# Redrawing the instruction order of an attention-and-MoE kernel: head, steady step, loads and tail at once

## The chip, the cores and the metric

One NeuronCore of a Trainium2 chip. Time is device time in microseconds (us), the median of several executions. The trace is of one execution under the hardware profiler. All executions that are compared are fast unless it is said. Ratios are the mean time of one kernel's fast runs over that of the other's of the same rounds, so they are not quite the ratio of the medians that are quoted. PE is TensorE, DVE VectorE, ACT ScalarE, POOL GpSimd, SP the engine whose queue issues the transfers.

## The reference

```python
f = 1 / (1 + exp(-f_logit))                       # 4 batches, 8 heads, 768 positions, 48 wide
for t in range(S):
    state = f[:, :, t, :, None] * state + outer(k[:, :, t], v[:, :, t])
    y[:, :, t] = q[:, :, t] @ state               # per head
x  = y as [3072 tokens, 384]
out = maximum(x @ w1, x @ w2) @ w_out             # d_ff = 1024
```

## The kernel before

The sequence is cut into 24 steps of 128 positions of one batch. The maximum is rewritten as x @ w2 plus relu(x @ (w1 - w2)), so the kernel prepares `wd = w1 - w2` and `w2o = w2 @ w_out` once, at the start, and every step then runs the same short list of operations. An operation of step i is written as a name and a number; a text lists them in program order, and each engine takes its own in that order. Who waits for whom follows from the data.

```python
PROLOGUE = """setup 0 ... lf 1 lf 0 lq 0 ... """      # head, written out
STEP     = """st -4  d0 -1  cum 1  a 0  ed 1 ... """  # step i; the number is added to i
EPILOGUE = """ ... """                                # tail, written out

# loads (SP): lf lk lq lv of f, k, q, v, 192 KB each, nine buffers of each; out: a store
# ACT:  e, ln (log of the gate), ei, ed (exp of the running sum), fl, x, g0, g1 (relu)
# PE:   cum, tr (transposes of kp and qp), a (scores), y, xT, sa, d0, d1 (x @ wd), o0, o1 (into out)
# DVE:  am (scores x mask), tre, xTe, ob (out of PSUM), tmp, v (v to bf16), w2Te
def m_kp(i, eng):                                     # kp = k * ei; "kp" on POOL, "kpv" on DVE
    eng.tensor_mul(s["kp"][:, :, 0:D], ld[i]["k"], s["ei"]...)
def m_qp(i, eng):                                     # qp = q * ed; "qp" on POOL, "qpv" on DVE
    eng.tensor_mul(s["qp"][:, :, 0:D], ld[i]["q"], s["ed"]...)
def m_st(i):                                          # state, two halves, always on POOL
    nc.gpsimd.tensor_mul(st_b[...], tmp[...], fl[...])
def sub_wd(j, eng=nc.vector):                         # "wd" on DVE, "wdp" on POOL
    eng.tensor_sub(wd[:, j, :], w1_f[:, j, :], w2_f[:, j, :])
def v_v(i):
    nc.vector.tensor_copy(vb, ld[i]["v"]...)          # f32 to bf16
```

## Time and profile before

| | before |
|---|---|
| time | 146.09 us (145.61 to 146.18) |
| PE busy | 130.0 us of a span of 144.2 |
| step in the steady part | 4.975 us, PE never idle |
| last idle time of PE before that part | 0.61 us, at y of step 3 |
| DMA | 28.3 MB in 129 transfers, busy from the second slice on |

How to read it: PE sets the end from 37 us on. What can change the time is when PE becomes dense, and whether something breaks it afterwards. The prediction below shows the lines.

### The profile page before, as it was taken

To read this page: it belongs to the slowest core of one execution; us is meant where nothing else is said; L and a number is where in the kernel's file an instruction comes from. 1 tells how busy PE (TensorE), PEld (TensorE's weight loads), DVE (VectorE), ACT (ScalarE), POOL (GpSimd) and SP (SyncE) were. 2 spreads that over 40 slices of the span, in tenths; PEclk is the share of its full clock that TensorE was granted. 3 is DMA by queue.
4 is the path that set the end of the run, shared out by engine and by line. 5 is a ranking of instruction groups with operands and counts; after the bars stand their busy time and mean duration, and the time that the engine had idled before them with its cause. 6 is when DMAs were issued, how large, how long until landed. Compare 5 with 4: busy or idle time off the path is not lost.

```text
span 144.2 us, 4442 instructions
## 1 busy us (share of the span) xinstructions
PE 130.0 (90%) x1820; PEld 101.3 (70%) x1820; DVE 104.4 (72%) x191; ACT 88.6 (61%) x199; POOL 54.6 (38%) x80
## 2 busy tenths in 40 slices
PE   0197499999899999999999999999999999999981
PEld 0044366677678877887887788778878877777771
DVE  7234988766989778877977797798779777976520
ACT  3572548877387566658566765766585667663440
POOL 8320060230556066236524632652364246362000
PEclk9999999999999999999999999999999999999999
DMA  4999999999999999999898999989899998971111
GB/s 93 271 362 386 341 303 154 188 188 140 206 174 196 188 213 221 173 227 233 166 203 183 215 208 210 219 181 196 182 198 222 190 251 180 225 223 57 59 55 55
DMA packets 104612, 28.60 MB, mean 198 GB/s; under 512 B 100368, under 2 KB 103568, under 8 KB 104592
## 3 DMA queue, kind: packets, MB, share of 16 engines
q1 hardware_dynamic: 104592, 28.32, 90.1%
q8 instruction: 14, 0.23, 0.7%
q14 instruction: 6, 0.05, 0.1%
HBM read 23.59 MB, written 4.72 MB: 196 GB/s over the span
## 4 chain that ended last, share of the span: by engine, by line
PE 72%; SPq 19%; DMA 4%; DVE 1%; issue 1%; ACT 0%
PE o L352 25%; PE d L334 22%; SPq L148 13%; PE tr L249 6%; PE a L267 5%; SPq L153 5%; DMA vt<-in_v_dram 4%; PE y L312 3%; PE y L307 2%; PE xtp L322 2%; PE cum L214 2%; PE sa L281 2%; SPq L157 1%; PE o L373 1%; DVE am L272 1%
## 5 line engine op out<-in xcount | busy, mean ns | idle before, releaser
L242 POOL TENSOR_TENSOR qp<-qt,ed 128x384 bf16<-128x384 f32 x22 | 22.3, 1013 | 61.7 <-ACT ed L226 31.6
L334 PE MATMUL d<-xT,wd 128*128 128x128 bf16 x576 | 40.6, 220 | 0.8 <-DVE xT L326 0.4
L352 PE MATMUL o<-wo,gT 128*128 128x384 bf16 x184 | 37.4, 325 | 0.0
L334 PEld LDWEIGHTS <-wd 128*128 128x128 bf16 x576 | 34.4, 114 | 3.8 <-DVE wd L175 0.6
L341 ACT ACTIVATE gT<-d 128x512 bf16<-128x512 f32 x48 | 29.0, 604 | 10.1 <-PE d L334 10.0
L272 DVE TENSOR_TENSOR am<-a,mask 128x1024 bf16<-128x1024 f32 x24 | 29.4, 1224 | 0.7 <-PE a L267 0.7
L296 POOL TENSOR_TENSOR st<-tmp,fl 64x192 bf16<-64x192 f32 x40 | 25.5, 638 | 1.6
L326 DVE COPY xT<-xtp 128x384 bf16<-128x384 bf16 x24 | 8.6, 358 | 21.1 <-PE xtp L322 21.1
L352 PEld LDWEIGHTS <-gT 128*128 128x128 bf16 x184 | 16.1, 97 | 9.1 <-ACT gT L341 0.2
L226 ACT ACTIVATE ed<-cum 128x384 f32<-128x384 f32 x24 | 11.8, 493 | 16.5 <-PE cum L216 13.1
L258 DVE COPY trs<-tr 128x1024 bf16<-128x1024 bf16 (+1 forms) x27 | 17.0, 631 | 2.9 <-PE tr L249 1.1
L317 ACT CAST x<-y 128x384 bf16<-128x384 f32 x24 | 11.5, 478 | 12.3 <-PE y L312 12.3
L352 PE MATMUL o<-w2o,xT 128*128 128x384 bf16 x69 | 15.0, 326 | 0.0
L201 ACT ACTIVATE e<-ft 128x384 f32<-128x384 f32 x24 | 12.5, 525 | 3.4 <-DMA ft<-in_f_logit_dram 3.4
L237 DVE TENSOR_TENSOR kp<-kt,ei 128x384 bf16<-128x384 f32 x23 | 14.1, 613 | 0.5 <-ACT ei L222 0.5
L214 PE MATMUL cum<-ell,ut 128*128 128x384 bf16 x24 | 8.1, 340 | 6.8 <-ACT ell L205 6.8
L205 ACT ACTIVATE ell<-e 128x384 bf16<-128x384 f32 x24 | 12.5, 524 | 0.7
L357 DVE COPY ob<-o 128x384 f32<-128x384 f32 x23 | 12.6, 548 | 0.0
L222 ACT ACTIVATE ei<-cum 128x384 f32<-128x384 f32 x24 | 12.1, 503 | 0.0
L312 PE MATMUL y<-vb,am 128*128 128x48 bf16 x192 | 11.3, 183 | 0.8 <-DVE am L272 0.6
L312 PEld LDWEIGHTS <-am 128*128 128x128 bf16 x192 | 9.6, 96 | 3.1 <-DVE am L272 1.4
L289 DVE TENSOR_TENSOR tmp<-sa,st 128x384 f32<-128x384 f32 x20 | 10.9, 546 | 0.0
(56 smaller groups left out, 167.6 us busy)
## 6 DMA issues: line engine op xcount, KB each, us to landing
ft<-in_f_logit_dram SPq DMA_DIRECT2D x24, 192.0 KB, 4.2
qt<-in_q_dram SPq DMA_DIRECT2D x24, 192.0 KB, 4.6
kt<-in_k_dram SPq DMA_DIRECT2D x24, 192.0 KB, 4.2
vt<-in_v_dram SPq DMA_DIRECT2D x24, 192.0 KB, 4.5
out_dram<-ob SPq DMA_DIRECT2D x23, 192.0 KB, 3.6
w_f<-in_moe_w_dram SPq DMA_DIRECT2D x6, 512.0 KB, 6.9
wo_f<-in_moe_w_out_dram SPq DMA_DIRECT2D x2, 768.0 KB, 8.4
out_dram<-obl SPq DMA_DIRECT2D x2, 96.0 KB, 1.6
```

The source lines that it names most:

```text
L148: nc.sync.dma_start(out=t, in_=SRC[name][b, :, sl, :].rearrange("h p d -> p h d"))
L201: nc.scalar.activation(e, ld[i]["f"].rearrange("p h d -> p (h d)"), AF.Exp, scale=-1.0)
L237: eng.tensor_mul(s["kp"][:, :, 0:D], ld[i]["k"], s["ei"].rearrange("p (h d) -> p h d", h=H))
L242: eng.tensor_mul(s["qp"][:, :, 0:D], ld[i]["q"], s["ed"].rearrange("p (h d) -> p h d", h=H))
L258: nc.vector.tensor_copy(s["tr"][:, n:n + len(sel)], psum.pop(("tr" + sel, i)))
L272: nc.vector.tensor_mul(am.rearrange("p o n c -> p (o n) c"), psum.pop(("a", i)).rearrange("p o n c -> p (o n) c"), mask)
L296: nc.gpsimd.tensor_mul(st_b[b][(c + 1) % 2][r, :, e], st[i]["tmp"][r, :, e], st[i]["fl"][r, :].unsqueeze(2).to_broadcast([DP, NP, D]))
L312: nc.tensor.matmul(out=y[:, ds], lhsT=am[:, o, p, :], rhs=vb[:, ds], start=(c == 0), stop=(c == 0 or o == 1))
L334: nc.tensor.matmul(out=ps[:, n, :], lhsT=wd[:, j, ff(f)], rhs=st[i]["xT"][:, j, :], start=(j == 0), stop=(j == JG - 1))
L341: nc.scalar.activation(s["g"][:, half * 4:half * 4 + 4, :], psum.pop(("d", half, i)), AF.Relu)
L352: nc.tensor.matmul(out=psum["o", i], lhsT=l() if callable(l) else l, rhs=r, start=(n == 0), stop=(n == len(mms) - 1))
L357: nc.vector.tensor_copy(t, psum.pop(("o", i)))
```

## The change

Its intent: draw the orders of all engines anew for the head (seven steps), the steady step and the tail, around the same first sixteen loads (the two loads of w_out trade places) and with their landing times from the trace. No operation of the kernel changes; nine `warm` matmuls, which kept the array busy early, go. The texts differ in nearly every line; the parts that matter are:

```diff
 PROLOGUE   (cut; ... marks cuts)
-... cum 0  cum 1  lw1 0  w2ca 2  warm 5 ... warm 3  warm 1 ... w2ca 1  w2T 0 ...
+... cum 0  ei 0  ln 1 ... w2ca 2 ... w2c 0  lq 1  w2c 1  kpv 0  w2T 5 ... w2T 1  w2Te 4  cum 1 ...
-... lf 3  wdp 0  woc 3  xT 0  trke 1  w2o 5  xTe 0 ... wd 2 ... wd 1
+... tmp 0 ... st 0 ... kp 1 ... wdp 0 ... wd 2  xT 0 ... xTe 0 ... wd 1
-... qp 2 ... kpv 2 ... kpv 3 ... qp 3 ... qp 4 ... kpv 4 ... qp 5 ... kpv 5
+... qp 2 ... kpv 2 ... kp 3  g1 1  v 2 ... qpv 3 ... qp 4 ... kp 4 ... kp 5 ... qp 5
-... lf 5 ... lv 3  lq 4  lk 4  lk 5  lv 4  lq 5  lv 5 ... lf 9  out 0  lv 8  out 1  lk 9
+... lv 3  lq 4  lk 4  lf 5  lv 4  lv 5  lk 5 ... lf 11  lv 7  lq 8  lf 10  lk 8  lq 10  lq 9  lv 11  lv 8  lk 9
 STEP
-st -4  d0 -1  cum 1  a 0  ed 1  d1 -1  g0 -1  am 0  lv 2  qp 1  fl 1  ei 1  lq 3  g1 -1
-o0 -1  kpv 1  y 0  tmp -2  lk 3  o1 -1  x 0  e 2  xT 0  tr 1  ln 2  out -4  xTe 0  sa -1
-tre 1  ob -1  lf 4  v 1
+st -4  cum 1  d0 -1  ei 1  a 0  g0 -1  d1 -1  am 0  fl 1  g1 -1  o0 -1  tmp -2  ed 1  y 0
+e 2  kpv 1  o1 -1  x 0  qpv 1  ln 2  xT 0  tr 1  xTe 0  sa -1  tre 1  ob -1  v 1  lv 5  lq 7
+lk 7  out -4  lf 9
 EPILOGUE
-(five steps written out) ... lo 0  lo 2  lob0 0  lo 1 ... lo 3  lout 0  lob1 0 ... lout 1
+... lo 1  lo 3  lob1 0  lo 0  lo 2  lout 1  lob0 0  lout 0
```

More of the change, by code (lines that the diff above doesn't have):

```diff
@@ L17 @@
 PROLOGUE = """
-setup 0  setup 2  setup 1  lf 1  lf 0  lq 0  lw2 2  lk 0  lw2 0  lw2 1  lv 0  lwo 0  e 0
-lwo 1  e 1  ln 1  lk 1  ln 0  cum 0  cum 1  lw1 0  w2ca 2  warm 5  ei 0  lw1 2  fl 0  ed 0
-kp 0  ei 1  qpv 0  ed 1  fl 1  lw1 1  w2c 0  warm 3  warm 1  lq 1  w2ca 1  w2T 0  lf 2  w2T 7
-trk 0  w2Te 7  trq 0  w2T 4  trke 0  w2Te 0  trqe 0  w2T 5  w2T 1  a 0  lv 1  am 0  w2Te 1
-w2Te 4  v 0  lq 2  woc 2  w2T 2  y 0  w2Te 2  w2Te 5  woc 0  w2T 6  lk 2  w2T 3  woc 1  w2Te 6
-w2o 2  kpv 1  w2o 1  x 0  w2Te 3  trk 1  lf 3  wdp 0  woc 3  xT 0  trke 1  w2o 5  xTe 0
@@ L24 @@
-w2o 4  w2o 7  w2o 10  lv 2  w2o 8  w2o 0  sa 0  wd 2  w2o 11  w2o 3  lk 3  w2oe 2  w2o 6
-w2oe 1  w2o 9  wd 1  w2oe 0  lq 3  qpv 1  d1 0  lf 4  e 2  trq 1  d0 0  ln 2  trqe 1  tmp 0
-lf 5  a 1  g0 0  v 1  cum 2  am 1  ed 2  lv 3  o0 0  g1 0  qp 2  ei 2  y 1  fl 2  lq 4  kpv 2
-o1 0  x 1  xT 1  trk 2  xTe 1  lk 4  e 3  trq 2  trke 2  d0 1  ln 3  trqe 2  ob 0  lk 5
-cum 3  a 2  v 2  ed 3  d1 1  g0 1  am 2  lv 4  ei 3  g1 1  o0 1  kpv 3  lq 5  y 2  qp 3
-o1 1  x 2  fl 3  xT 2  lv 5  e 4  tr 3  xTe 2  ln 4  sa 1  d0 2  tre 3  lf 6  ob 1  cum 4
@@ L30 @@
-g0 2  a 3  d1 2  ed 4  lk 6  v 3  am 3  ei 4  g1 2  o0 2  lq 6  qp 4  e 5  tmp 1  y 3  fl 4
-o1 2  x 3  st 0  lf 7  kpv 4  ln 5  xT 3  tr 4  xTe 3  sa 2  lk 7  cum 5  tre 4  d0 3  ob 2
-a 4  lv 6  v 4  g0 3  d1 3  am 4  ei 5  ed 5  lv 7  g1 3  o0 3  qp 5  tmp 2  fl 5  y 4  kpv 5
-lq 7  o1 3  x 4  st 2  xT 4  lq 9  e 6  tr 5  xTe 4  st 1  sa 3  ln 6  d0 4  tre 5  lf 8
-ob 3  cum 6  g0 4  a 5  v 5  d1 4  ed 6  am 5  lq 8  ei 6  qp 6  g1 4  o0 4  tmp 3  fl 6
-out 2  e 7  y 5  kpv 6  o1 4  x 5  lk 8  ln 7  xT 5  tr 6  xTe 5  sa 4  lf 9  d0 5  tre 6
@@ L36 @@
-ob 4  cum 7  g0 5  a 6  out 0  v 6  d1 5  ed 7  am 6  ei 7  lv 8  qp 7  g1 5  o0 5  tmp 4
-y 6  kpv 7  out 1  o1 5  x 6  st 3  fl 7  xT 6  tr 7  lk 9  e 8  xTe 6  sa 5  ln 8  tre 7
-lk 10  ob 5  v 7  lf 10
+setup 0  setup 2  setup 1  lf 1  lf 0  lq 0  lw2 2  lk 0  lw2 0  lw2 1  lv 0  lwo 1  e 0
+lwo 0  e 1  ln 0  lk 1  cum 0  ei 0  ln 1  lw1 0  ed 0  w2ca 2  lw1 2  lw1 1  w2c 0  lq 1
+w2c 1  kpv 0  w2T 5  lf 2  w2T 4  w2Te 5  w2T 1  w2Te 4  cum 1  qpv 0  w2T 3  ed 1  tr 0
+lv 1  w2Te 3  woc 3  v 0  w2Te 1  w2T 6  ei 1  tre 0  w2T 2  fl 1  fl 0  sa 0  w2Te 6  w2T 0
@@ new lines @@
+tmp 0  lq 2  woc 0  w2T 7  w2Te 0  a 0  st 0  w2Te 7  woc 1  w2Te 2  lk 2  w2o 2  am 0  woc 2
+kp 1  w2o 1  w2o 0  lf 3  w2o 3  wdp 0  y 0  trk 1  x 0  w2o 4  w2o 5  lk 3  wd 2  xT 0
+w2o 8  w2o 7  w2o 11  xTe 0  w2o 6  lv 2  wd 1  w2oe 2  w2o 10  w2o 9  w2oe 1  lq 3  qpv 1
+w2oe 0  d1 0  trke 1  trq 1  lf 4  e 2  d0 0  trqe 1  ln 2  a 1  g0 0  lv 3  v 1  cum 2
+am 1  fl 2  g1 0  o0 0  lq 4  ed 2  ei 2  y 1  qp 2  lk 4  o1 0  x 1  kpv 2  xT 1  trk 2
+lf 5  e 3  xTe 1  trq 2  trke 2  d0 1  ln 3  trqe 2  ob 0  lv 4  a 2  g0 1  cum 3  am 2
@@ new lines @@
+d1 1  fl 3  ei 3  lv 5  kp 3  g1 1  v 2  o0 1  lk 5  ed 3  y 2  qpv 3  o1 1  x 2  lf 6  e 4
+xT 2  tr 3  ln 4  xTe 2  sa 1  lq 5  d0 2  tre 3  ob 1  cum 4  lf 7  a 3  v 3  ed 4  d1 2
+g0 2  am 3  qp 4  lk 7  ei 4  fl 4  g1 2  o0 2  tmp 1  kp 4  lq 6  e 5  y 3  o1 2  x 3  st 1
+ln 5  lk 6  v 4  xT 3  tr 4  xTe 3  cum 5  tre 4  d0 3  lf 8  ei 5  ob 2  sa 2  a 4  g0 3
+v 5  lv 6  d1 3  kp 5  ed 5  am 4  lq 7  e 6  o0 3  g1 3  tmp 2  y 4  out 2  qp 5  o1 3
+x 4  fl 5  xT 4  st 2  lf 9  e 7  tr 5  xTe 4  ln 6  sa 3  d0 4  tre 5  lf 11  ob 3  cum 6
@@ new lines @@
+a 5  tmp 3  ed 6  lv 7  d1 4  g0 4  am 5  fl 6  ln 7  lq 8  ei 6  o0 4  qpv 6  g1 4  y 5
+kp 6  lf 10  o1 4  x 5  st 3  xT 5  tr 6  lk 8  xTe 5  cum 7  tre 6  d0 5  ei 7  lq 10  ob 4
+fl 7  sa 4  a 6  g0 5  lq 9  v 6  d1 5  ed 7  am 6  e 8  qp 7  lv 11  g1 5  o0 5  kpv 7
+ln 8  y 6  lv 8  tmp 4  o1 5  x 6  e 9  lk 9  xT 6  tr 7  xTe 6  cum 8  tre 7  d0 6  lf 13
+ob 5  sa 5  a 7  v 7  lv 9  lq 11  lq 12  out 0  lk 10  lq 14  lv 10  lf 12  lk 11  lk 12
+lv 12  out 1  out 5  out 4  lf 14  lf 15  lq 13  lk 14  lk 13
@@ L47 @@
 EPILOGUE = """
-st 15  d0 18  cum 20  a 19  ed 20  d1 18  g0 18  am 19  qp 20  ei 20  lv 21  g1 18  o0 18
-tmp 17  st 16  out 15  y 19  kpv 20  o1 18  x 19  lk 22  e 21  xT 19  tr 20  ln 21  xTe 19
-sa 18  d0 19  tre 20  lq 22  ob 18  cum 21  a 20  ed 21  v 20  lf 23  d1 19  g0 19  am 20
-qp 21  ei 21  g1 19  lv 22  o0 19  tmp 18  st 17  fl 21  out 16  y 20  kpv 21  o1 19  x 20
-lk 23  e 22  xT 20  tr 21  xTe 20  ln 22  sa 19  d0 20  tre 21  lq 23  ob 19  cum 22  lv 23
-a 21  ed 22  v 21  d1 20  g0 20  am 21  ei 22  out 17  g1 20  o0 20  tmp 19  fl 22  y 21
-out 18  qp 22  kpv 22  o1 20  x 21  st 18  xT 21  out 19  e 23  tr 22  xTe 21  ln 23  sa 20
-d0 21  tre 22  st 22  st 23  st 19  ob 20  cum 23  a 22  g0 21  v 22  d1 21  out 20  ed 23
-am 22  ei 23  g1 21  o0 21  tmp 20  kpv 23  y 22  qp 23  o1 21  x 22  xT 22  st 20  st 21
-tr 23  xTe 22  sa 21  d0 22  tre 23  ob 21  a 23  g0 22  v 23  d1 22  out 21  am 23  g1 22
-o0 22  tmp 21  y 23  o1 22  x 23  xT 23  sa 22  xTe 23  ob 22  d0 23  out 22  d1 23  g0 23
-sa 23  g1 23  lo 0  lo 2  lob0 0  lo 1  fl 23  lo 3  lout 0  lob1 0  tmp 22  tmp 23  lout 1
+st 21  st 20  st 23  st 22  tmp 23  tmp 22  lo 1  lo 3  lob1 0  lo 0  lo 2  lout 1  lob0 0
+lout 0
 """
```

## The prediction

> **What bounds the kernel now.** The page first, for the shares.
>
> ```profile
> span 144.2 us, 4442 instructions
> PE 130.0 (90%) x1820; PEld 101.3 (70%) x1820; DVE 104.4 (72%) x191; ACT 88.6 (61%) x199; POOL 54.6 (38%) x80
> PE   0197499999899999999999999999999999999981
> DMA  4999999999999999999898999989899998971111
> ```
>
> TensorE is full from a seventh of the span on, and so are the DMA engines: two resources run side by side. The gaps in TensorE lie in the first ten slices (3.6 us each). The busy time by windows confirms it (window, then PE, PEld, DVE, ACT, POOL, clock, DMA share, GB/s):
>
> ```profile
> 15.00:20.00 5.00, 3.34 (x35) 2.33 (x36) 4.42 (x12) 3.42 (x5) 1.73 (x1) 1.00 1.07 360
> 20.00:25.00 5.00, 4.68 (x56) 3.36 (x55) 4.34 (x6) 2.75 (x6) 0.63 (x1) 1.00 1.09 172
> 35.00:40.00 5.00, 4.39 (x64) 3.15 (x62) 4.41 (x8) 2.46 (x7) 2.16 (x3) 1.00 0.95 176
> 60.00:100.00 40.00, 40.00 (x606) 32.69 (x606) 31.76 (x57) 26.95 (x66) 18.27 (x24) 1.00 0.98 201
> ```
>
> From 40 us TensorE is never idle, so a new order can't shorten that part; it can only start it earlier, or break it. A step takes 4.97 us there. The chain of waits up to 37 us shows the last thing that held it:
>
> ```profile
> 28.15 0.94 SPq L148
> 29.13 6.07 DMA vt<-in_v_dram
> 35.26 0.24 issue
> 35.50 1.23 DVE am L272
> ```
>
> It runs through the issue of loads from the start and leaves it only when v of step 3 lands at 35.2 us; behind that stand its cast, the mask product am 3 and y 3. The TensorE timeline gives the price, and the gap where d begins:
>
> ```profile
> 22.90 0.81 PE L334 MATMUL d<-xT,wd 128*128 128x128 bf16 x11 [0.32 <-DVE wd L175]
> ...
> 36.78 0.37 PE L312 MATMUL y<-vb,am 128*128 128x48 bf16 x8 [0.61 <-DVE am L272]
> ```
>
> After 22.90 TensorE loses that 0.61 us, some 0.1 us at y 1, and 0.45 us in the tail. So the accounting is: the end moves by (start of the dense d, less 22.90), less at most 0.71, plus new stalls.
>
> **What the Trainium skill says.** "TensorE: Matmul & The Clock Gate", Part 1: an idle array runs at half clock (107 ns between 128-column matmuls, 56 when warm) until about one 3.4 us window of work has passed. The trace agrees: the 512-column warm matmuls are 0.43 us apart until 11 us, the 128-column ones later 0.056. "SBUF — State Buffer", Who interferes with whom: a VectorE instruction with two SBUF inputs and a GpSimd one that reads SBUF exclude each other for the whole instruction. The trace agrees; the tile view of the weights (ns, min/median/max) has
>
> ```profile
> L175 DVE TENSOR_TENSOR wd<-w_f x2: 1212/1676/2140, 19.6 to 21.6; 128x1024 bf16<-128x1024 f32 x2
> L175 POOL TENSOR_TENSOR wd<-w_f x1: 2353/2353/2353, 18.3 to 18.3; 128x1024 bf16<-128x1024 f32 x1
> ```
>
> POOL held 18.27 to 20.62; wd 2 began on DVE at 19.57 and ended at 21.71, 1.09 after POOL let go; wd 1 alone took 1.21. "DMA: Bandwidth & Descriptors", Specifications, asks for 512 B or more for full rate. Of this kernel's 104,612 packets 100,368 are smaller, and loads of 192 KB land 0.95 to 1.1 us apart (some 190 GB/s), weights of 512 KB 1.3 us apart.
>
> **The change part by part.** The instructions are the same, but for nine warm matmuls (4.0 us at a time when TensorE had nothing to do; worth 0 in themselves) and for which engine does what: the third w2 cast goes from ACT to DVE, qp goes to DVE in nearly all steps, kp to POOL in some early ones.
>
> (a) Start of w2. Weight w2 1 lands at 11.15. Its cast was 1.04 on ACT with transposes from 12.27; on DVE it takes 0.68, so transposes start at 11.9: 0.4 earlier. But without warm they run cold: 3 x 0.107 = 0.32 us per w2T in place of 0.17. Eight of them, with tr 0, sa 0 and a 0 among them, end near 16.7. The last eviction (w2Te 2) is then at 17.25, so w2o starts at 17.3 in place of 17.66. The swap of the two wo loads puts woc 3 at 14 and leaves only three casts behind the landing at 16.0, which end at 18.35. TensorE is through w2o at about 21.9, or 23 if the clock stays low until 18.7.
>
> (b) Start of d. It needs all three wd. POOL now has st 0 and kp 1 ahead of wdp 0. I get: cum 1 after three w2T at 13.4; ed 1, woc 3, ei 1, fl 1, fl 0 on ACT until 15.35; sa 0 (its PSUM buffer waits for fl 0) until 15.7; tmp 0 until 16.3; st 0 1.35 until 17.7; kp 1 1.0 until 18.7; wdp 0 2.35 until 21.05. By the lock, wd 2 ends at 21.05 + 1.09 = 22.1; xTe 0, now between, 0.36; wd 1 1.2. So d starts at about 23.65; at best, if kp 1 is done by the landing of w1 at 18.2, at 23.25. That is **0.35 to 0.75 us later** than 22.90.
>
> (c) v 3. It is the 25th transfer now, not the 26th: by the old landings 32.9, not 35.2. The 0.61 us go, and the shift of (b) is just repaid: y 3 at about 36.5 against 36.78.
>
> (d) What comes next in the queue. I give each load the landing of the same place in the old queue. f 5 (28th) lands at 36.6, and ACT has e 5 ahead of x 3: x 3 starts at 37.1, about as before (37.19). v 4 (29th) lands at 38.1 and stands on DVE ahead of xTe 3: d of step 3 waits until about 38.8 (before 38.86). q 5 is 33rd, not 31st: 42.2, not 40.05; qp 5 takes 1.0 on POOL, so the q half of tr 5 can't run before 43.3; it ran at 43.21, its k half at 42.99. So every gain above ends here, with **+0.1 to +0.3 us** on the old time.
>
> (e) Steady step. DVE gets qp. Its row of a step was am 59.98, kp 61.12, tmp 61.61, then 0.94 idle until xT at 63.09. With qp (0.5) after kp, the idle time is 0.45. qp needs ed, which ACT now does after g1: 60.94 + 0.45 + 0.49 = 61.9, in time; kp ends at 62.1 and qp at 62.65, before tr at 63.06. x starts at 62.2 in place of 62.11 and ends 0.2 before TensorE wants it. cum, moved before d0, needs ln by 63.67 and has it at 63.1. Worth **0**: TensorE stays the bound at 4.97 us.
>
> (f) Loads run up to nine steps ahead, not four. That costs places early: k 10 is 58th, not 51st. From the 49th at 56.97 with 0.96 each it lands at 65.6; kp 10 wants it at 66.56. v 8 is 51st, about 58.9, wanted at 59.65. Tight, no stall. (g) The tail swaps the halves of the last output and their engines (0.32 and 0.36 us): **0**.
>
> Sum: 146.09 + 0.2 = 146.3 us.
>
> **The rivals.** First: the new order gains. If DMA lands faster than place by place (the hole from 32.9 to 35.2 is no law), q 5 and f 5 come up to 1.5 us sooner, and if wdp 0 gets its turn at 18.2, d loses 0.35 only; then the end moves by 0.35 - 0.71 - up to 0.4: 145.2 to 145.7. More is hardly there, as everything before 22.1 waits for w1 to land at 20.91 plus 1.2 of wd 1. For it speaks that the landings went into the new order.
>
> Second: the lock breaks the steady step. st on POOL follows tmp and so falls between kp and qp. One half of st takes 0.64; if it slips in, qp ends at about 63.25, and the q half of tr, due at 63.28, is late by about 0.05. Against it: in the steady part of before kp beside st took 0.56, and st gave way. If it happens in all 17 steps, 0.05 to 0.1 each: 147 to 148.
>
> Third: the clock. Without warm the window that frees it may pass a stretch with too many gaps. Then w2o runs cold (24 x 0.32 = 7.7 us in place of 3.9), d starts at about 26 and the time is 148 to 149. Against it: between 11.9 and 16.7 TensorE would be at work in most of each window, as cold matmuls fill it better.
>
> Fourth: DMA takes over as the bound. 129 transfers, some 112 of them after 22 us at 0.96: done by about 130, ahead of TensorE's 141. It can hold single steps, not the whole.
>
> **Range and chances.** Between 145.2 (first rival) and 148 (second, or a little of the third) most outcomes lie; 146.3 is the likeliest. Range 144.9 to 148.0. Faster than 143.2 would need 2.9 us, more than the 0.71 us of idle time after d and the 0.8 us before it that the landing of w1 allows: 0.05. Slower than 149.0 needs the cold clock or the lock at full size: 0.07. Within: 0.88.
>
> **What would show it.** The first dense d at 23.2 to 23.7 with DVE wd as its releaser, wdp 0 on POOL at 18.2 to 18.7, and wd 2 ending 1.1 after it; y 3 without an idle time of 0.6; an idle time of TensorE before tr 5 or d 0 of step 3 that leads to the landing of q 5 or v 4; steps of 4.97 us from 50 to 135 with xT's idle time on DVE at about 0.45. Wrong would be: dense d before 22.5; TensorE idle in the steady part (lock or landings); w2o matmuls 0.32 us apart.

## The result, and the profile after

The changed kernel takes 147.51 us (147.13 to 147.68, 4 runs), the kernel before 145.97 in the same rounds (145.61 to 146.18): ratio 1.0104, 95% interval 1.0074 to 1.0134. One per cent slower is clear of the noise.

The page after has the same shape: PE is full, a little later; DVE has more to do, POOL less.

```profile
span 145.9 us, 4442 instructions
PE 127.9 (88%) x1811; PEld 101.0 (69%) x1811; DVE 117.2 (80%) x205; ACT 88.6 (61%) x198; POOL 41.6 (29%) x66
```

PE's busy time fell by 2.1 us, yet the span grew by 1.7: the `warm` matmuls (4.0 us) went, which stood at a time when PE had nothing else to do, and other matmuls take longer in sum. The PE timeline shows where PE waited between the start of d and the steady part (start, duration, what, and in brackets the idle time before it and who ended it):

```profile
24.07 0.81 PE L325 MATMUL d<-xT,wd 128*128 128x128 bf16 x11 [0.82 <-DVE wd L166]
...
29.07 0.40 PE L240 MATMUL tr<-ident,kp 128*128 128x128 bf16 x4 [0.29 <-DVE kp L228]
...
33.00 0.37 PE L303 MATMUL y<-vb,am 128*128 128x48 bf16 x8 [0.27 <-DVE vb L200]
...
42.66 0.21 PE L298 MATMUL y<-st,trs 128*128 128x96 bf16 x1
42.99 0.22 PE L303 MATMUL y<-vb,am 128*128 128x48 bf16 x2
```

The 0.61 us before y 3 are gone, as intended; new waits stand before tr 2, in y 2 and in y 4 (0.33 us between its first two matmuls, where the later ones follow in about 0.05), and d starts 1.17 us later than before (22.90). POOL and DVE at the start of d:

```profile
18.22 1.00 POOL L228 TENSOR_TENSOR kp<-kt,ei 128x384 bf16<-128x384 f32 x1
19.18 2.35 POOL L166 TENSOR_TENSOR wd<-w_f 128x1024 bf16<-128x1024 f32 x1
```

```profile
20.14 2.48 DVE L166 TENSOR_TENSOR wd<-w_f 128x1024 bf16<-128x1024 f32 x1 [1.33 <-DMA w_f<-in_moe_w_dram]
22.54 0.34 DVE L317 COPY xT<-xtp 128x384 bf16<-128x384 bf16 x1
22.80 1.21 DVE L166 TENSOR_TENSOR wd<-w_f 128x1024 bf16<-128x1024 f32 x1
```

GpSimd's subtraction queues behind kp 1 and ends at 21.53; the first on DVE, which began beside it, ends at 22.62, 1.09 later, the distance that the kernel before showed. Now the new waits. The same DVE, and POOL, in steps 1 to 4:

```profile
27.94 1.07 DVE L228 TENSOR_TENSOR kp<-kt,ei 128x384 bf16<-128x384 f32 x1 [0.58 <-ACT ei L213]
...
31.89 1.05 DVE L200 CAST vb<-vt 128x384 bf16<-128x384 f32 x1
...
40.72 1.08 DVE L200 CAST vb<-vt 128x384 bf16<-128x384 f32 x1
```

```profile
27.60 1.00 POOL L233 TENSOR_TENSOR qp<-qt,ed 128x384 bf16<-128x384 f32 x1 [6.07 <-ACT ed L217]
31.73 1.00 POOL L228 TENSOR_TENSOR kp<-kt,ei 128x384 bf16<-128x384 f32 x1 [3.13 <-ACT ei L213]
...
40.57 1.01 POOL L228 TENSOR_TENSOR kp<-kt,ei 128x384 bf16<-128x384 f32 x1 [0.89 <-ACT ei L213]
```

In the kernel before, the cast of v 2 had GpSimd idle beside it:

```profile
29.11 0.35 DVE L209 CAST vb<-vt 128x384 bf16<-128x384 f32 x1
```

A product of 0.55 us took 1.07 and a cast of 0.35 us took 1.05 and 1.08, each time next to a GpSimd product that began up to 0.34 us sooner. This exclusion of VectorE and GpSimd is what the prediction calls the lock. PE waits for kp 2 and the cast of v 2 themselves, and for am 4, which stands behind the cast of v 5 in DVE's queue.

The steady part has no idle time, yet it is slower. In the window from 60 to 100 us PE (second column, with its instructions) does five fewer than before (606, in the prediction):

```profile
60.00:100.00 40.00, 40.00 (x601) 32.15 (x599) 37.75 (x64) 27.23 (x64) 11.34 (x16) 1.00 1.09 201
```

To add it all up I followed one landmark, the start of the scores `a` of each step, read from both traces:

| `a` of step | 1 | 2 | 3 | 4 | 5 | 8 | 18 | 23 |
|---|---|---|---|---|---|---|---|---|
| before, us | 24.53 | 29.19 | 34.00 | 39.63 | 44.61 | 59.54 | 109.31 | 133.65 |
| after, later by | 1.17 | 1.12 | 1.82 | 1.03 | 1.32 | 1.44 | 1.88 | 1.76 |

So: +1.17 at d, -0.05 and +0.70 over steps 1 and 2, -0.79 at step 3, +0.29 at step 4, then some 0.044 us a step, 0.56 from step 5 to 18. Steps 1 and 2 are to be read together, 0.65: cum 3 stands ahead of `a` 2 in the kernel before and behind it in the changed one, which moves about 0.3 us from one to the other. The experiments take these apart.

### The profile page after: what moved, and what is told of

Same layout as the page of the kernel before. It is cut to its first block, busy times and chain, and to the rows that moved or that the text cites. A ratio compares the mean times of both kernels' runs of the same rounds, so it can differ in the third digit from the quotient of the medians.

```text
span 145.9 us, 4442 instructions
## 1 busy us (share of the span) xinstructions
PE 127.9 (88%) x1811; PEld 101.0 (69%) x1811; DVE 117.2 (80%) x205; ACT 88.6 (61%) x198; POOL 41.6 (29%) x66
## 4 chain that ended last, share of the span: by engine, by line
PE 75%; SPq 8%; DVE 7%; DMA 5%; issue 2%; ACT 2%; DVEq 0%
PE o L343 26%; PE d L325 23%; PE tr L240 7%; PE a L258 5%; DMA w_f<-in_moe_w_dram 5%; SPq L144 4%; PE y L303 3%; PE xtp L313 3%; DVE wd L166 2%; PE y L298 2%; PE cum L205 2%; SPq L139 2%; PE sa L272 2%; SPq L148 2%; DVE vb L200 1%
## 5 line engine op out<-in xcount | busy, mean ns | idle before, releaser
L287 POOL TENSOR_TENSOR st<-tmp,fl 64x192 bf16<-64x192 f32 x40 | 26.2, 654 | 67.3 <-ACT ed L217 42.5
L213 ACT ACTIVATE ei<-cum 128x384 f32<-128x384 f32 x24 | 11.9, 495 | 17.3 <-PE cum L207 14.0
L233 DVE TENSOR_TENSOR qp<-qt,ed 128x384 bf16<-128x384 f32 x20 | 15.7, 783 | 0.0
L228 DVE TENSOR_TENSOR kp<-kt,ei 128x384 bf16<-128x384 f32 x19 | 11.3, 595 | 0.6 <-ACT ei L213 0.6
```

Source lines behind the costliest of these rows:

```text
L213: nc.scalar.activation(t, psum["cum", i][:, 0:dm], AF.Exp)
L233: eng.tensor_mul(s["qp"][:, :, 0:D], ld[i]["q"], s["ed"].rearrange("p (h d) -> p h d", h=H))
L287: nc.gpsimd.tensor_mul(st_b[b][(c + 1) % 2][r, :, e], st[i]["tmp"][r, :, e], st[i]["fl"][r, :].unsqueeze(2).to_broadcast([DP, NP, D]))
```

## The experiments

Twelve kernels, in three groups of four; the runs of one group share the chip and the runs of the kernel before (medians 146.06, 146.3 and 147.23; in the third group one run of the kernel before was slow and two fast ones had a granted clock of 0.975 and 0.988, so its ratios say little, and I compare within the group). Where runs of two groups are compared, it is across chips and rounds. Edits are to the changed kernel unless it is said.

**d0 ahead of cum again, in the steady step alone.**

```diff
-st -4  cum 1  d0 -1  ei 1 ...
+st -4  d0 -1  cum 1  ei 1 ...
```

> The changed kernel with one edit: in the steady step d0 goes ahead of cum on TensorE again, as in the kernel before. Theory: the step grew from 4.975 to 5.02 us only through this place of cum (the trace has +0.83 us on d and -0.57 on cum's small matmuls in eight steps), so the steps from 8 to 19 are back at 4.975 and the time falls by 0.4 to 0.6 us against the changed kernel. Rival (the longer step comes from the GpSimd lock on VectorE, late qp): no change of the step, 0.0 us.

Measured: 147.55 us (147.51 for the changed kernel, not of the same rounds): no gain in time. The trace shows one all the same. From step 8 to the end `a` stays 1.66 us behind the kernel before, in every step, where the changed kernel drifts from 1.44 to 1.88; in 60 to 100 us PE does

```profile
60.00:100.00 40.00, 40.00 (x608) 32.70 (x606) 37.80 (x65) 26.33 (x64) 11.21 (x16) 1.00 1.08 197
```

Per step, from one start of a matmul to the next, d and the small matmuls of cum take

```
us a step (steps 8 to 15)     before   changed   this run
d0 and d1 (24 matmuls)         1.368     1.472      1.367
cum, 384 columns               0.163     0.173      0.162
cum, four of one column        0.174     0.103      0.174
```

Entering `a` costs PE a pause. After the one-column matmuls it costs 0.07 us, after a d of 128 columns 0.10, and 0.01 goes to cum: 0.044 in all. (Leaving `a` costs 0.09 in all three. That the reason is the 48 rows of its operands, where all others have 128, is my guess; no run varies it.) That is the growth, and DVE has no part in it: DVE is as full in this run (37.80 of 40) as in the changed kernel (37.75). In this profile the head was later by 0.25 us (`a` of step 1; half of it from the first w1, which landed at 18.89, not 18.76), which hides most of the gain. Why the other five runs (146.67 to 148.53) show none in the median isn't known: they are not traced.

**kp 1 on VectorE, so that the GpSimd subtraction is not behind it.**

```diff
-kp 1  w2o 1  w2o 0  lf 3 ...
+kpv 1  w2o 1  w2o 0  lf 3 ...
```

> The changed kernel with kp 1 on VectorE in place of GpSimd, so that the GpSimd weight subtraction no longer queues behind it. Theory: that subtraction starts at the landing of the first w1 (18.2 to 18.8) in place of 19.18, the second one on VectorE ends 1.09 us after it, and the dense d starts 0.4 us sooner; the time falls by 0.2 to 0.4 us. Rival (the landing of the last w1 or the slower clock holds d): d does not move, 0.0 us.

Measured: 148.25 us (148.14 without the one slow run of the six); the profiled run took 147.57, so what made others 0.6 to 0.9 us longer isn't in its trace. In it d starts at 23.95, 5.40 us after the landing of the first w1 (5.31 in the changed kernel). A miss, even with the clock allowed for, which came at 17.46 us here and at 15.47 there: three runs below with the clock at 16.37 to 17.66 and without this edit have 5.44 to 5.46. POOL's line shows why:

```profile
18.67 2.74 POOL L166 TENSOR_TENSOR wd<-w_f 128x1024 bf16<-128x1024 f32 x1 [0.60 <-POOL st L287]
```

The subtraction started sooner, but kp 1 on DVE (18.65 to 19.20) now held the lock, and GpSimd took 2.74 us in place of 2.35. It ended at 21.41, hardly sooner than the 21.53 of the changed kernel. The lock works both ways, so moving an operation off GpSimd to the other party of the lock bought some 0.05 us here. My theory had counted GpSimd's queue and not the lock.

**The warm matmuls back.**

```diff
-ei 0  ln 1  lw1 0 ...
+ei 0  ln 1  warm 5  warm 3  warm 1  lw1 0 ...
```

> The changed kernel with the nine warm matmuls back in, behind cum 0. Theory: the clock is free at about 12 us in place of 15.47 and the transposes of w2 take half as long, but d waits for the weight subtraction, so the time changes by 0.0, at most -0.1 us. Rival (the cold clock delays d): d sooner by 0.3 us or more and the time with it.

Measured: 148.68 us, slower still, but d at 23.50, 4.95 us after the landing of the first w1. The full clock was granted at 11.70 us (12.05 in the kernel before, 15.47 in the changed one), the transposes of w2 and sa 0 came sooner, and with them st 0 and kp 1 on GpSimd, so its subtraction started at 18.62, with the landing. I had said that d wouldn't move; the rival was right about d, not about the time. Landings vary from profile to profile by some tenths (the first w1 from 18.20 to 18.89 behind the same eleven transfers, two of which trade places in the kernel before), so d has to be read from them:

| | before | changed | warm back |
|---|---|---|---|
| first w1 lands | 18.20 | 18.76 | 18.55 |
| dense d starts | 22.90 | 24.07 | 23.50 |
| difference | 4.70 | 5.31 | 4.95 |

The cold clock is worth 0.36 us of d's start (by some 0.1 more in the runs where it came later than 15.47), the rest of the order (xT's copy between the two subtractions, above all) 0.25, and 0.56 of the 1.17 in the traced pair is the luck of the landings. The time rose because of a wait that the changed kernel doesn't have: y of step 8 stood idle for 1.55 us, with v 8 landing at 62.68, 2.10 us behind v 11 where the changed kernel has 1.06. The trace shows a hole in the transfers between the two (the last columns are the clock, the DMA share and GB/s):

```profile
60.00:61.00 1.00, 1.00 (x22) 0.81 (x20) 0.63 (x2) 0.80 (x2) 0.00 (x0) 1.00 1.08 181
61.00:62.00 1.00, 1.00 (x15) 0.82 (x14) 0.00 (x0) 0.54 (x3) 0.00 (x0) 1.00 0.24 33
```

**No products of steps 2 to 7 on GpSimd.**

```diff
-qp 2 ... kp 3  g1 1  v 2 ... qp 4 ... kp 4 ... kp 5 ... qp 5 ... kp 6 ... qp 7
+qpv 2 ... g1 1  v 2  kpv 3 ... qpv 4 ... kpv 4 ... (am 4) kpv 5  qpv 5 ... kpv 6 ... qpv 7
```

> The changed kernel with all kp and qp of steps 2 to 7 on VectorE, none on GpSimd (kp 1 stays there). Theory: the waits of VectorE for GpSimd go (casts of v in steps 2 and 5 at 0.35 us in place of 1.05, kp 2 at 0.55 in place of 1.07), and with them TensorE's idle 0.29, 0.27 and about 0.3 us before tr 2, y 2 and in y 4: 0.5 to 0.9 us less. Rival (the landings of q and v hold these steps): the idle time stays, at other instructions, and the time changes by under 0.2 us.

Measured: 148.14 us, slower than the changed kernel. Yet in the trace the idle time is gone from tr 2, y 2 and y 4, the casts of v in steps 2 and 5 take 0.35 us, and `a` of step 8 is 0.38 us behind the kernel before in place of 1.44. Then, in one step, all of that and more is lost:

```profile
62.59 0.22 PE L303 MATMUL y<-vb,am 128*128 128x48 bf16 x2 [0.46 <-DVE am L263]
...
64.90 0.40 PE L240 MATMUL tr<-ident,qp 128*128 128x128 bf16 x4 [0.38 <-DVE qp L233]
```

```profile
61.04 0.36 DVE L200 CAST vb<-vt 128x384 bf16<-128x384 f32 x1 [0.98 <-DMA vt<-in_v_dram]
...
63.45 0.61 DVE L228 TENSOR_TENSOR kp<-kt,ei 128x384 bf16<-128x384 f32 x1 [0.45 <-DMA kt<-in_k_dram]
```

DVE waits for v 8, then for k 9: both are loaded behind f 11, f 10, q 10 and v 11, of which f 10 is first used at 62.01 us, f 11 and q 10 at 68.43 and 69.00, v 11 at 76.50. In the changed kernel's own profile v 8 had landed 0.19 us and k 10 0.09 us ahead of their use. Its loads and its compute were late by the same amount; I took this for the reason that a gain elsewhere couldn't show, and the second group tests it.

**The load order alone, put into the kernel before.** All other engines keep the order of the kernel before; only the transfers from the 17th on come in the order of the changed kernel (the diff of the change shows the core of it).

> The kernel before with only the order of loads and stores after the first sixteen taken from the changed kernel; every compute engine as before. Theory: v 8 lands at about 60.9 us and k 10 at about 68.1, where the kernel before wants them at 59.64 and 66.1, so TensorE idles in steps 8 to 10 and the time is 147.3 to 148.2 us: the load order alone makes the kernel as slow as the whole change. Rival (the load order is slack, the compute order costs): 146.1 us, or 145.5 as v 3 comes sooner.

Measured: the profiled run took 147.40 us, the other two fast ones 147.24 and 146.30; three were slow (149.30 to 150.02; what made them so isn't known, none was traced), so the median of all six, 148.35, isn't used. Ratio of the fast ones 1.0035 (0.9987 to 1.0083): in time not clear. In the trace it is: in steps 1 to 3 this kernel is 0.26 to 0.28 us behind the kernel before (the granted clock fell to half from 16.20 to 19.61 us), in steps 4 to 8 it is 0.16 to 0.37 us *ahead*, as the wait for v 3 is gone, and then

```profile
61.42 0.38 DVE L234 CAST vb<-vt 128x384 bf16<-128x384 f32 x1 [1.85 <-DMA vt<-in_v_dram]
```

```profile
62.98 0.22 PE L337 MATMUL y<-vb,am 128*128 128x48 bf16 x2 [1.39 <-DVE am L297]
```

after which it stays 1.41 behind to the end. Loading farther ahead with a full DMA is not free: each transfer that comes early puts off one that is due.

**The old load order under the GpSimd-free compute order.** My first mend: the kernel with no products of steps 2 to 7 on GpSimd, with the transfers from the 17th on as in the kernel before.

> The run without GpSimd products in steps 2 to 7 (148.14 us), with only the order of loads and stores after the first sixteen put back to that of the kernel before (nearest need first, no farther ahead). Theory: what that run gained by step 8 (its a was 0.38 us behind the kernel before there, against 1.44 in the changed kernel) was lost in steps 8 and 9 to v 8 and k 9 landing behind loads that nobody needs yet; with them in time the shift stays at 0.4 us and grows by 0.044 a step over twelve steps: 146.6 to 147.1 us. Rival (the longer queue of work on VectorE without GpSimd is what costs): no change, 148.1 us, with idle time of TensorE in steps 8 and 9.

Measured: 149.13 us median of five; the four fast ones lie between 148.68 and 149.16. A miss, and taken alone it speaks against the theory. (The fifth, the profiled one, took 327.82 us: matmuls of 384 columns were 0.43 us apart until 300 us, against 0.16. The clock reads 1.00, but only because this trace, like that of the first experiment, holds no clock record at all. I don't know what that was, and use nothing of its trace.) The next run, traced, suggests why.

**The same with d0 ahead of cum.**

> As the run with need order, and d0 ahead of cum on TensorE again in all steps. Theory: the growth of 0.044 us a step goes too: 146.0 to 146.5 us. Rival: as the run with need order, within 0.1.

Measured: 148.84 us (148.62 over the four fast ones). Its trace has no wait in steps 8 to 10 any more, but two early ones: 0.80 us at d0 of step 3, behind v 4, and 1.56 us at cum 7, behind f 7:

```profile
39.40 0.77 PE L359 MATMUL d<-xT,wd 128*128 128x128 bf16 x11 [0.80 <-DVE xT L351]
```

```profile
45.99 0.52 ACT L226 ACTIVATE e<-ft 128x384 f32<-128x384 f32 x1 [2.27 <-DMA ft<-in_f_logit_dram]
```

```profile
46.98 0.32 PE L239 MATMUL cum<-ell,ut 128*128 128x384 bf16 x1 [1.56 <-ACT ell L230]
```

The new compute order takes e 7 earlier than the old one (ahead of ln 6), and the old load order brings f 7 later. An order of loads is good only for the compute order that it was drawn with, and I had exchanged one without the other. The load order had to be mended, not replaced.

**The kernel before, with v 3 sooner and wd 0 on VectorE.** v 3 and f 5 trade places (the expectation's "two places" is one), and `trke 1` goes behind wd 1.

```diff
 (kernel before)
-lf 3  wdp 0  woc 3  xT 0  trke 1 ... wd 1  w2oe 0 ... lf 5  a 1 ... lv 3
+lf 3  wd 0   woc 3  xT 0         ... wd 1  trke 1  w2oe 0 ... lv 3  a 1 ... lf 5
```

> The kernel before with two edits that the comparison suggests: v 3 is loaded two places sooner (in place of f 5), and the first weight subtraction goes from GpSimd to VectorE, so that the three run there one after the other without the lock. Theory: the idle 0.61 us before y 3 goes, and d starts at about 22.5 in place of 22.90: 145.0 to 145.5 us. Rival (the loads hold both): 146.0 us.

Measured: 146.25 us, ratio 1.0008 (0.9969 to 1.0047): no gain. Both edits did what they should: dense d starts at 22.48, and nothing waits before y 3. The gain went at y 1, and 0.40 us more at tr of step 4:

```profile
25.18 0.36 DVE L209 CAST vb<-vt 128x384 bf16<-128x384 f32 x1 [0.73 <-DMA vt<-in_v_dram]
```

v 1 can't be cast before it lands, and PE then idles 0.86 us at y 1. (v 1 landed at 25.16 here and at 24.68 in the kernel before, so up to half of that is the spread of the landings.) What stood behind the subtraction stands behind the load instead. The head of the kernel before was balanced to within half a microsecond.

**The later loads by need, the early ones kept.** The third group keeps the first 41 transfers of the changed kernel and sorts those after them by need: v 8 is the 46th (51st in the changed kernel), k 9 the 48th (52nd), k 10 the 53rd (58th). The first of them has no products of steps 2 to 7 on GpSimd.

```diff
-... lf 9  lf 11  lv 7  lq 8  lf 10  lk 8  lq 10  lq 9  lv 11  lv 8  lk 9  lf 13  lv 9 ...
+... lf 9  lv 7  lq 8  lk 8  lv 8  lq 9  lk 9  lf 10  out 0  lv 9  lq 10  lk 10  lf 11  out 1 ...
```

> The run without GpSimd products in steps 2 to 7 (148.14 us) with its own first 41 transfers, and the later loads and stores sorted by need (v 8 46th in place of 51st, k 9 48th in place of 52nd, k 10 53rd in place of 58th). The run with need order fell because the early part of the old order (v 5, f 6, f 7 later) does not fit this compute order; here the early part stays. Theory: v 8 lands at about 55 to 56 us, no idle time of TensorE in steps 8 to 10, so the shift stays at 0.3 to 0.5 us at step 8 and grows by 0.044 a step: 146.6 to 147.2 us. Rival (something else in steps 8 and 9 costs): 148.1 us.

Measured: **146.42 us** (146.24 to 146.68), against 148.14 with the same compute order and loads far ahead. (The two are of different groups and chips; the traces below don't depend on it.) `a` of step 8 is at 59.54, that of the kernel before to the hundredth, and v 8 lands at 54.99. The drift of 0.044 a step follows as expected.

**The changed kernel with the later loads by need, and nothing else.**

> The changed kernel with only its loads and stores after the first 41 sorted by need. Theory: in the profile of the changed kernel v 8 landed 0.19 us, k 10 0.09 us ahead of use, so the order of loads holds it only in some runs: 147.0 to 147.5 us, 0.0 to 0.5 less than the changed kernel. Rival (the landings are its bound from step 8 on): 146.5 us or less.

Measured: 147.62 us, against 147.51: no gain. So the order of the loads is not what makes the changed kernel slow. It hides behind the compute order: only where the compute is faster does it hold. These two runs are of one group and differ in the GpSimd products alone: 147.62 - 146.42 = **1.20 us** is their price. The two traces agree, and as PE runs the same list in both they can be compared matmul by matmul: from `a` of step 1 to that of step 8 the one with the products falls back 1.2 us, 0.33 of it before tr 2, 0.44 at y 2 and 0.30 in y 4, each time released by DVE and not by GpSimd. Another 0.10, before xT of step 3, is f 5, which landed at 37.89 us in one and at 36.44 in the other. So the lock's part is about 1.05 to 1.1 us. With the loads far ahead the same edit had made the kernel slower, 148.14 against 147.51.

**The same as the first of this group, with d0 ahead of cum in all steps.** In the written-out steps 3, 5 and 6 too.

> The run before it with d0 ahead of cum again in all steps. Theory: the growth over the steps goes, 0.4 to 0.6 us less: 146.1 to 146.6 us, no different from the kernel before by more than 0.4%. Rival: as the run before it.

Measured: 146.64 us; not the gain that I expected. The drift is gone (`a` is 0.60 us behind from step 8 to the end), but between steps 3 and 8 this kernel lost 0.6 us to the one without the swap. It goes at the three places where d0 was moved in the head: over d0 and cum of steps 3, 5 and 6 `a` falls back by 0.26, 0.15 and 0.15 us. There d0 came to stand right behind the transposes, and started some 0.05 us after DVE ended the copy of xT each time (at 38.67, 48.81 and 53.98 us), where cum had filled the gap; the profile's list of idle times shows only the first, as 0.17. The swap pays in the steady step and costs in these head steps. Both together, as the traces add up (0.00 at step 8 from one run, no drift from the other), would tie with the kernel before; it wasn't run.

**The same with the warm matmuls.**

> As the run with loads by need and d0 first, with the nine warm matmuls back. In the run with warm alone d started 0.57 us sooner than in the changed kernel (0.2 of it from the landings), as the state and key products got to GpSimd sooner; then v 8 took it back. Theory: 0.2 to 0.4 us below the run before it: 145.8 to 146.4 us, the time of the kernel before. Rival (later loads hold it again): as the run before it.

Measured: 146.75 us, against 146.64: not resolved in time. In the trace d starts 4.95 us after the first w1 (5.32 without), just as with warm alone, and the end is 0.19 us nearer to the kernel before. 0.13 of the gain at d was lost to the later landing in this profile.

Summed up, with `a` behind the kernel before (us):

| run | step 1 | step 3 | step 5 | step 8 | step 18 | median time |
|---|---|---|---|---|---|---|
| changed | 1.17 | 1.82 | 1.32 | 1.44 | 1.88 | 147.51 |
| d0 first, steady step | 1.42 | 2.08 | 1.58 | 1.66 | 1.66 | 147.55 |
| warm back | 0.61 | 1.26 | 0.83 | 0.95 | 3.27 | 148.68 |
| no GpSimd products | 0.97 | 0.85 | 0.27 | 0.38 | 2.27 | 148.14 |
| old kernel, loads ahead | 0.28 | 0.26 | -0.16 | -0.16 | 1.41 | (147.24, fast runs) |
| later loads by need | 1.02 | 1.67 | 1.35 | 1.48 | 1.91 | 147.62 |
| both of these mends | 0.75 | 0.63 | -0.11 | 0.00 | 0.43 | 146.42 |

(Each row is one execution, and landings differ between executions by some tenths, so the rows are better read along than against each other.) No version beats the kernel before by more than the noise.

## Why the prediction was right or wrong

The measured 147.51 lies in the range (144.9 to 148.0). The sum was too small: +0.2 us foretold, +1.5 measured. That the range held it is luck as far as the mechanism goes: the range reached up to 148 for the second rival, and PE never waited as that rival said. Step by step:

(a) Start of w2: right. Transposes run cold; w2o starts at 17.42 us (17.3 foretold) and its last matmul at 22.12 (21.9), with w2 1 landing 0.53 later than in the old trace.

(b) Start of d: right in kind, low as it stands: d at 24.07, outside the 23.2 to 23.7 that were to show it, and GpSimd's subtraction at 19.18, not 18.2 to 18.7. DVE's subtraction is the releaser, and the end 1.09 us after GpSimd lets go came out to the hundredth. I gave +0.35 to +0.75; with the 0.56 us of landing luck taken out it is +0.61. The chain to kp 1 had the cold transposes of (a) in it, but not their share set apart: it is 0.36, and what remains is xT's copy, which I had at 0.36 and which cost 0.25.

(c) v 3: right. It landed at 33.2, and the idle time before y 3 is gone. "The shift of (b) is just repaid" is wrong: y 3 starts at 37.82, not 36.5, as d came later than foretold and the waits of (d) followed.

(d) Early steps: **this term failed**. "So every gain above ends here, with +0.1 to +0.3 us" put the limit at the landings of f 5, v 4 and q 5. They landed as said (36.3, 38.2, 42.1), but what held PE was the lock of (b) in other places: the cast of v 2 and v 5, and kp 2, at 1.05 to 1.08 us beside a GpSimd product. I had the lock in hand, with its size, and applied it only to the subtractions and, as a rival, to st beside qp; kp 2 beside qp 2 and the casts of f32 to bf16 I left out. Measured by the one pair of runs that differs in this alone, with loads that don't hold, it is 1.20 us, some 1.05 to 1.1 of it the lock. Of the three landings, that of v 4 kept DVE idle for 0.31 us in the changed kernel, but no idle time of PE leads to it.

(e) Steady step: also mis-sized. "Worth 0" was argued for DVE and ACT, and they do have the room: DVE's idle time before xT is 0.18 us, not 0.45, as qp takes 0.86 between the halves of st, but PE doesn't wait. What I left out was PE itself: I took an order of matmuls to cost the sum of its parts. The way into `a` costs 0.044 us more in the new order, over twelve steps 0.5 us. The second rival had the size ("147 to 148") for a wrong reason: not the lock but the order of PE.

(f) Loads far ahead: "Tight, no stall" was right for this kernel, by 0.09 and 0.19 us, and by luck: v 8 and k 10 landed at 60.85 and 68.05 us, 2.0 and 2.4 after the foretold 58.9 and 65.6, and only because the compute was 1.4 us late itself did nobody wait. As a general statement it is useless: of the six kernels with this load order that were traced (the changed one, d0 first, kp 1 on VectorE, warm back, no GpSimd products, the old kernel with loads ahead), three stalled at step 8 or 9, by 1.55, 0.84 (0.46 and 0.38) and 1.39 us.

(g) Tail: right, no difference beyond the order of the last steps (1.88 to 1.76, by 0.12 us).

The terms as measured in the trace: d 1.17 (0.56 of it landings), steps 1 and 2 0.65 (the lock's two waits, less what else changed there), v 3 and the rest of step 3 -0.79, lock in step 4 0.29, drift 0.56, tail -0.12: together 1.76, against 1.77 between the ends of PE (142.98 and 141.21). What stays open: what makes the holes in the transfers, and the run of 328 us. v 8 lands anywhere from 60.1 to 62.7 us at the same place of the queue, latest in the two traces with a hole just ahead of it: 33 GB/s from 61 to 62 us with the warm matmuls, 41 from 60 to 61 in the old kernel with loads ahead, where about 180 is usual.

## What to carry to other kernels

When two engines exclude each other, as VectorE and GpSimd do here, list *every* instruction of both that can be held, casts too, and check each pair that an order makes neighbours; an operation moved from one to the other can still meet the lock from the other side, as kp 1 did. When DMA is near its limit, prefetching one thing is postponing another: sort by need, and test a load order only with the compute order that it was made for. And read experiments by a landmark per step, not by the time alone: four of these runs (warm back, no GpSimd products, the old kernel with loads ahead, and with v 3 sooner) gained at one place and lost it again to a later wait.

## What the Trainium skill lacked or had wrong

- "SBUF — State Buffer", Who interferes with whom, is right and goes further than I used it: it counts copies and casts in VectorE's two-port modes among those that GpSimd blocks. Here a cast of 128x384 from f32 to bf16 took 1.05 and 1.08 us beside a GpSimd product, 0.35 alone. The lock held GpSimd up as well: 2.74 us in place of 2.35.
- No page has a number for the pause between matmuls of 128 rows and of 48; the subject belongs to "TensorEngine Tiling (Array Packing)". Here the entry into `a` costs 0.10 us after a 128-column matmul and 0.07 after one-column ones, 0.044 us a step by order alone (that the rows are the reason is not shown).
- "TensorE: Matmul & The Clock Gate", Part 1, says that the cold start is under 1% of a typical kernel. The runs agree: 0.36 us at the start of d, 0.19 us at the end. It also warns that the clock's record can't always be trusted; no run here shows a wrong record, but two traces have none, and their clock then reads 1.00, the run of 328 us among them, with matmuls 0.43 us apart, against 0.16.
- "DMA: Bandwidth & Descriptors" asks for 512 B or more and gives no rate for rows of 192 B: here 192 KB in such rows landed every 0.95 to 1.1 us. No page has the spread of a landing from run to run: the first w1 landed at 18.20 to 18.89 us behind the same eleven transfers.
